# One step over four PSUM banks for the tails' u of the last pair of batches

## The chip, the cores and the metric

The kernel runs on one core of a Trainium2 chip. The metric is the device time of one execution in microseconds. The engines are PE (matmuls, with its weight loads PEld), DVE and ACT (element-wise work, both read PSUM), POOL (element-wise work and DMA issue) and SP (DMA issue). PSUM has eight banks of 128 partitions by 512 float32; here they are called g0, g1, g2, o0, o1, T and X (X is two banks side by side).

## What is computed

Cosformer attention over 8 batches, 8 heads, 576 positions and 64 features a head, and behind it a mixer: a low-rank mixing over positions and two large products.

```
def phi(x, c, s):
    r = np.maximum(x, 0.0)
    return np.concatenate([r * c, r * s], axis=-1)
...
kv = np.einsum('bhsf,bhsd->bhfd', k_p, v)
num = np.einsum('bhsf,bhfd->bhsd', q_p, kv)
...
xt = x.transpose(0, 2, 1)
h = xt @ U @ V                       # U 576 x 32, V 32 x 576
u = x + h.transpose(0, 2, 1)
ch = np.maximum(u @ w_ch1, 0.0) @ w_ch2    # 512 -> 2048 -> 512
return (u + ch).astype(np.float32)
```

## The kernel before

**Tiling.** The 576 positions of a batch are four blocks of 128 and a tail of 64. The tails of two batches share one tile of 128 rows: the even batch has the lower 64 partitions, the odd one the upper. For each batch the attention gives x (512 columns), A = (x' U) as four row strips of 32 (one for each block of 128 columns), and u = x + (V-product of A). The main blocks' u is made by `u_mm` and `u_add`, the tails' u of a pair by `u_tail`; u is then transposed by a DMA from SP (`utr_dma`, L522 and L528) and goes into the first large product.

**`u_tail` (L489 to 507).** For a set of column blocks `js` it takes one PSUM bank for each, from `four_banks` (L458): the two halves of X first, then the spare banks that the caller names. For each of the two batches and each column block it issues one matmul of 32 rows by 64 columns of weights and 128 columns of data (L498), and then one DVE addition for each column block (L505), which reads the bank and writes the block of `u_tl`. `u_tl` is transposed by SP, and its reader on PE is the tails' first product (`g1_tail`, L722).

**The order of the work** is written out by hand: a list of slots (`slots`), each a bit of PE work, and thunks that are put behind a slot (`put`); `attention_plan(b)` puts the attention of batch b at slots counted from w. For the last batch w is 187 and `a_at` is 14, so the tails' u stands behind slots 210 and 212. Every engine works through its own instructions in the order in which they are issued here; the waits between engines are found from the tiles.

**What stands around slot 210.** The first product of batch 6 (and 7) is done here with seven products of quarter size in place of eight (`g1_cross`, L650 to 681; `g1_join`, L683 to 710), for column blocks p of 128. Batch 6's blocks 4 to 7 are made this way. Products 1, 6, 7 and 4 add up in half a bank called X of that group (g0 or g1), 2 in the other half (Y), and products 5 and 3 in a bank called Z, which for batch 6 is always bank T. Joins on ACT and DVE read them: P1 and P5 (ACT copies X and Z to SBUF), C11 (DVE adds P1 and Y), C22 (DVE adds P5 and X), U2 (ACT copies X), R21 and R22 (ACT), C12 (DVE adds U2 and Z, and then takes the maximum with 0, L699). So T is taken by product 5 of block p, read by P5, taken by product 3, read by C12, and taken by product 5 of block p + 1. Between two groups of such products stand eight matmuls of the second product of batch 5 (`half_part`, L894, 128 x 256), joined by `more` (DVE, L850).

The slots are: 209, products 3 and 4 of block 5 and product 6 of block 6; 210, a `half_part`; 211, products 1 and 2 of block 7 and products 5 and 7 of block 6; 212, a `half_part`; 213, products 3 and 4 of block 6 and product 6 of block 7; 214, a `half_part`; 215, products 5 and 7 of block 7. Behind slot 209 also stands half of a sum of weights (`w1_sum`, a DVE subtraction of 128 x 1024, `w_s<-w_bf,w_s` at L612) for batch 7.

In the kernel before, the tails' step behind slot 210 has column blocks 0, 1 and 2 in X and g2 (tag "s"), and the step behind slot 212 has column block 3 in X.

```
def opened(b, p):
    g1_cross(b, p, 1)
    g1_cross(b, p, 2)
    g1_join(b, p, "P1")
    g1_join(b, p, "C11")
...
of_x, of_z = CROSS[p % 2] if b == B - 1 else (("g0", "g1")[p % 2], "T")
```

Of the kernel before, what the change touches and what calls it, by code (L numbers as in the profile page):

```python
# [17 lines left out]
def kernel(  # L18
# [28 lines left out]
    def tail(b):  # L47
        lo = TS * (b % 2)
        return slice(lo, lo + TS)
# [290 lines left out]
    def kv_unit(b, hg, tag, bufs, eng=None, n=E):  # L340
        if b not in kv_sb:
            kv_sb[b] = pool.tile([P, H, E], BF16, tag="kv", bufs=2, name="kv")
        acc = ps.tile([P, 4, n], FP32, tag=tag, bufs=bufs, name="kv_ps")
        vx = v_ext
        for i in range(4):
            h = hg * 4 + i
            for c in range(5):
                nc.tensor.matmul(  # L348
                    out=acc[:, i, :],
                    lhsT=k_of(b, c, h),  # L350
                    rhs=v_tl[:, h, 0:n] if c == 4 and b < NE
                    else vx[:, c if c < 4 else 4 + b % 2, h, 0:n],
                    start=(c == 0),
                    stop=(c == 4),
                )
        cast(eng or V_, kv_sb[b][:, hg * 4 : hg * 4 + 4, 0:n], acc)
# [83 lines left out]
    def A_of(b):  # L440
        return A_sb[b % 4]
# [16 lines left out]
    def four_banks(*spare):  # L458
        t = ps.tile([P, 2, 512], FP32, tag="X", bufs=1, name="va4_ps")
        more = [  # L460
            x if not isinstance(x, tuple)
            else ps.tile([P, 512], FP32, tag=x[0], bufs=x[1], name="va_ps")
            for x in spare
        ]
        return [t[:, 0, :], t[:, 1, :]] + more
# [3 lines left out]
    def u_mm(b, *spare, js=range(4)):  # L469
        if b not in u_bf:  # L470
            u_bf[b] = pool.tile([P, 4, 4, P], BF16, tag="u_bf", bufs=3, name="u_bf")
        va.setdefault(b, {}).update(zip(js, four_banks(*spare)))
        for c in range(4):
            for j in js:
                rows = slice(j * R, j * R + R)
                nc.tensor.matmul(  # L476
                    out=va[b][j][:, c * P : c * P + P], lhsT=V_bf[rows, c, :],
                    rhs=A_of(b)[rows, :], start=(c == 0), stop=(c == 3),
                    tile_position=(j * R, 0),
                )  # L480
# [5 lines left out]
            in1=va[b][j].rearrange("p (c n) -> p c n", c=4), op=ALU.add,  # L486
        )

    def u_tail(pr, *spare, js=range(4)):  # L489
        if pr not in u_tl:  # L490
            u_tl[pr] = pool.tile(
                [P, DM], BF16, tag="k_p" if pr == 3 else "u_tl", bufs=1, name="u_tl"
            )
        vt = dict(zip(js, four_banks(*spare)))
        for i in range(2):
            for j in js:
                rows = slice(j * R, j * R + R)
                nc.tensor.matmul(  # L498
                    out=vt[j][tail(i), 0:P], lhsT=V_tl[rows, :],
                    rhs=A_of(2 * pr + i)[rows, :], start=True, stop=True,  # L500
                    tile_position=(j * R, i * TS),
                )
        for j in js:
            ns = slice(j * P, j * P + P)
            nc.vector.tensor_tensor(  # L505
                out=u_tl[pr][:, ns], in0=x_tl[:, ns], in1=vt[j][:, 0:P], op=ALU.add
            )
# [465 lines left out]
    def loads(b):  # L973
        def thunk(dst, src):
            def go():
                if b < NE and dst is not qst:
                    load_even(dst, src, b)
                    load_odd(dst, src, b)
                    return
                load_tail(dst, src, b)  # L980
                load_main(dst, src, b)

            return go

        return thunk(qst, q), thunk(kst, k), thunk(vst, v)
# [3 lines left out]
    def spare(at):  # L989
        if at < 70:  # L990
            return ("o", 2) if 32 <= at < 52 else ("g", 3)
        return ("o", 2) if at < 86 else ("s", 1)
# [14 lines left out]
    def attention_plan(b):  # L1007

        plan = []
        if b < 4:  # L1010
            w, f_at, q_eng, k_eng, qtr, lo = PLAN[b]
        else:
            w, q_at, k_at, qtr, lo = PLAN[b]

        def put(at, f, *a, tag=False):
            if tag:
                a = a + spare(w + at)
            plan.append((w + at, lambda: f(b, *a)))

        for n, c in enumerate(QORD):  # L1020
            if b > 3:
                put(q_at[0] + q_at[1] * n, q_prep, c, q_at[2:])
                put(k_at[0] + k_at[1] * n, k_prep, c, k_at[2:])
                put(k_at[0] + (3 * n) // 2, v_prep, 0, H, (c,), (G_,))
                continue
            if b == 3:
                q_eng, k_eng = V_ if n == 3 else A_, A_ if n < 3 else None
                put((-15, -14, -13, -2, -6)[n], q_prep, c, (q_eng, q_eng))
                put(n - 12 if n < 3 else -8, k_prep, c, (A_, k_eng))
                if n > 2:  # L1030
                    put(-4, k_prep, c, (None, V_))
                put((-9, -9, -9, -7, -5)[n], v_prep, 0, H, (c,), (A_ if n > 2 else G_,))
                continue
            put(f_at + ((n - 1) % 5 if b == 2 else n), q_prep, c, (q_eng, q_eng))
            put(f_at + 6 + n, k_prep, c, (k_eng, k_eng))
            put((-5, -2, -1, -5, -5)[n], v_prep, 0, H, (c,), (V_ if n > 2 else A_,))
        for n, (c0, c1) in enumerate(((4, 5), (0, 2), (2, 4))):
            at = qtr[n] if b > 4 else -2 if b == 3 and n == 2 else qtr + 2 * n
            put(at, qtr_dma, c0, c1)
        plan.append((w + (b == 2), lambda: kv_unit(b, 0, *spare(w), A_)))  # L1040
        plan.append((w + 2, lambda: kv_unit(b, 1, *(T1 if b == 3 else spare(w + 2)), A_)))
        for n, c in enumerate(ORD):
            if b > 3:
                put((3 if b == B - 1 else 4) + 2 * n, x_unit, c, "X", 1)
            else:
                at = 4 + n if b == 3 else 4 + (3 * n) // 2
                if n % 2:
                    put(at, x_two, c, tag=True)
                else:
                    put(at, x_unit, c, "X", 1)  # L1050
        a_at = (12, 10)[b - 2] if b < 4 else 14
        if b == B - 1:
            put(a_at, A_unit, "s", 1, A_)
        else:
            put(a_at, A_unit, tag=True)
        odd = b % 2 == 1


        def two(at):
            return [T1, ("s", 1) if at >= 86 else G3] if at >= 86 or at < 64 else [spare(at)] * 2  # L1060

        if b == B - 1:
            plan.append((w + a_at + 2, lambda: u_mm(b, ("s", 1), js=(0, 1, 2))))
            plan.append((w + a_at + 5, lambda: u_mm(b, js=(3,))))
        else:
            u_at = w + a_at + (1 if b == 3 else 2)
            plan.append((u_at, lambda: u_mm(b, *two(u_at))))
        for j in range(4):
            n = (j + 1) // 2 if b == 2 else j // 2 - 1 if b == 3 else j + (2 if b > 4 and j > 1 else 0)
            put(a_at + 2 + n, u_add, j)  # L1070
        put(a_at + (2 if b == 3 else 3), utr_dma, 0, 2)
        put(a_at + (7 if b > 4 else 3 if b == 3 else 5), utr_dma, 2, 4)
        if odd:
            if b == B - 1:
                plan.append((w + a_at + 9, lambda: u_tail(b // 2, ("s", 1), js=(0, 1, 2))))
                plan.append((w + a_at + 11, lambda: u_tail(b // 2, js=(3,))))
            else:
                at = w + a_at + (10 if b == 5 else 8 if b == 3 else 9)
                plan.append((at, lambda at=at: u_tail(b // 2, *two(at))))
            put(a_at + (11 if b > 4 else 9 if b == 3 else 10), utr_dma, 4, 5)  # L1080
        for at, t in zip(lo, loads(b + 1) if lo else ()):
            plan.append((w + at, t))
        return plan
# [44 lines left out]
    T1 = ("T", 1)  # L1128
# [437 lines left out]
    for b in range(2, B):  # L1566
        for at, t in attention_plan(b):
            put(at, t)
# [37 lines left out]
```

## Time and profile before

| | |
|---|---|
| median of 3 runs | 290.36 us (290.25 to 290.58) |
| the profiled execution | 290.29 us |
| its span | 288.5 us |
| PE busy | 281.9 us, 98% |
| DVE busy | 212.0 us, 73% |
| ACT busy | 169.2 us, 59% |
| POOL busy | 64.7 us, 22% |
| granted PE clock | 0.999 |

The span runs from the first to the last event on the core; the profiled execution's own time is 1.8 us longer. Busy times of engines overlap. A row of a timeline gives the start, the length, the engine, the line and the operation, output and input names, and how many instructions were merged into the row; neighbouring instructions of one engine overlap in it, since each is shown with its whole length through the engine's pipeline. A bracket at the end of a row gives the idle time ahead of it and what ended it. The chain of work that ended last is followed back from the last instruction, and counts each stretch of time once.

### The profile page before, as it was taken

What the parts mean: (1) busy time and instruction counts of PE and PEld (TensorE: products, weight loads), DVE (VectorE), ACT (ScalarE), POOL (GpSimd) and SP (SyncE); (2) the same over time, 40 slices, a digit from 0 to 9 for tenths busy, and PEclk for the clock granted to TensorE, in tenths of its full rate; (3) what the DMA queues carried; (4) which work ended last, traced back from release to release, by engine and by line L of the source; (5) the groups of instructions that cost most, each with busy time, mean ns of one, the idle gap of its engine ahead of it and who ended that gap; (6) DMA issues with size and microseconds to landing.
All of it is one profiled execution on the core that took longest, in us unless ns stands there. A gap on an engine that the chain in (4) does not pass through costs nothing.

```text
span 288.5 us, 7416 instructions
## 1 busy us (share of the span) xinstructions
PE 281.9 (98%) x2961; PEld 199.0 (69%) x2992; DVE 212.0 (73%) x515; ACT 169.2 (59%) x347; POOL 64.7 (22%) x98
## 2 busy tenths in 40 slices
PE   8999999999999999999999999999999999999995
PEld 4785564446788546776766666766777889889884
DVE  5977858896876888557547794669968787775763
ACT  2955752177893557577735964497644556657310
POOL 6520500000046103302400501024201313303330
PEclk9999999999999999999999999999999999999999
DMA  7999999999999999998699939993930754436113
GB/s 225 306 254 250 278 160 192 225 328 220 363 252 202 272 248 256 203 332 207 175 227 268 245 74 250 180 339 91 183 77 9 140 120 82 88 96 112 39 75 143
DMA packets 92933, 56.17 MB, mean 195 GB/s; under 512 B 56580, under 2 KB 89732, under 8 KB 92900
## 3 DMA queue, kind: packets, MB, share of 16 engines
q1 hardware_dynamic: 82020, 43.41, 60.5%
q0 software_dynamic: 10688, 12.09, 20.7%
q8 instruction: 23, 0.38, 0.5%
q10 hardware_dynamic: 192, 0.20, 0.2%
q14 instruction: 10, 0.08, 0.1%
HBM read 36.86 MB, written 9.44 MB: 160 GB/s over the span
## 4 chain that ended last, share of the span: by engine, by line
PE 85%; DMA 8%; DVE 2%; ACT 2%; issue 1%; DVEq 0%; ACTq 0%
PE h_ps L894 32%; PE g_ps L580 26%; PE c_ps L677 7%; DMA kst<-in_k_dram 6%; PE o_ps L762 6%; PE gt_ps L722 5%; PE kv_ps L348 3%; PE x_ps L423 3%; DMA qst<-in_q_dram 2%; PE h_ps L762 1%; PE a_ps L446 1%; PE va_ps L476 1%; DVE k_p L309 1%; ACT q_p L307 1%; DVE v_ext L132 1%
## 5 line engine op out<-in xcount | busy, mean ns | idle before, releaser
L580 PE MATMUL g_ps<-uT,w_bf 128*128 128x512 bf16 x378 | 95.5, 379 | 1.1
L589 ACT ACTIVATE hid<-g_ps 128x512 bf16<-128x512 f32 x104 | 61.4, 597 | 59.7 <-PE g_ps L580 57.2
L580 PEld LDWEIGHTS <-w_bf 128*128 128x128 bf16 x402 | 37.5, 98 | 33.7
L894 PEld LDWEIGHTS <-hid 128*128 128x128 bf16 x560 | 53.0, 98 | 10.7
L894 PE MATMUL h_ps<-w_bf,hid 128*128 128x256 bf16 x336 | 43.1, 273 | 0.1
L894 PE MATMUL h_ps<-w_s,S 128*128 128x256 bf16 x240 | 30.4, 273 | 0.0
L894 PE MATMUL h_ps<-w_s,hid 128*128 128x256 bf16 x224 | 29.0, 273 | 0.0
L850 DVE TENSOR_TENSOR o_sb<-o_sb,h_ps 128x256 f32<-128x256 f32 (+1 forms) x38 | 16.9, 446 | 13.7 <-PE h_ps L894 11.2
L953 POOL DMA_DIRECT2D out_dram<-o_sb x20 | 12.9, 646 | 60.8 <-DVE o_sb L850 48.3
L894 PEld LDWEIGHTS <-S 128*128 128x128 bf16 x240 | 23.1, 98 | 4.9
L850 DVE TENSOR_TENSOR o_sb<-u_bf,h_ps 128x256 f32<-128x256 bf16 x32 | 13.3, 416 | 14.8 <-PE h_ps L894 14.6
L132 POOL CAST v_ext<-vst 128x512 bf16<-128x512 f32 (+1 forms) x22 | 16.0, 755 | 33.1 <-DMA vst<-in_v_dram 29.8
L484 DVE TENSOR_TENSOR u_bf<-x_bf,va_ps 128x512 bf16<-128x512 bf16 x27 | 17.6, 680 | 5.2 <-PE va_ps L476 4.1
L612 DVE TENSOR_TENSOR hid<-kept,c_ps 128x256 bf16<-128x256 f32 x36 | 14.7, 417 | 8.3 <-ACT kept L130 4.6
L952 POOL DMA_DIRECT2D o_sb<-u_bf x8 | 10.4, 1301 | 32.4 <-DVE rec L414 15.5
L130 ACT ACTIVATE kept<-c_ps 128x256 f32<-128x256 f32 x36 | 12.6, 384 | 7.2 <-PE c_ps L677 7.2
L722 PE MATMUL gt_ps<-uT_tl,w_bf 128*128 128x128 bf16 x256 | 16.2, 219 | 0.0
L433 DVE TENSOR_TENSOR x_bf<-x_ps,rec 128x512 bf16<-128x512 f32 x22 | 15.2, 692 | 0.8
L722 PEld LDWEIGHTS <-w_bf 128*128 128x128 bf16 x256 | 15.1, 98 | 0.7
L762 PE MATMUL o_ps<-w_bf,hid 128*128 128x512 bf16 x61 | 14.6, 379 | 0.3 <-issue 0.2
L130 ACT ACTIVATE o_sb<-h_ps 128x256 f32<-128x256 f32 x24 | 9.2, 381 | 9.4 <-PE h_ps L894 8.7
L307 ACT ACTIVATE k_p<-kst,cosw 128x512 bf16<-128x512 f32 x20 | 14.2, 713 | 0.1
(189 smaller groups left out, 459.5 us busy)
## 6 DMA issues: line engine op xcount, KB each, us to landing
qst<-in_q_dram SPq DMA_DIRECT2D x14, 512.0 KB, 5.8
kst<-in_k_dram SPq DMA_DIRECT2D x12, 512.0 KB, 7.4
out_dram<-o_sb POOLq DMA_DIRECT2D x21, 256.0 KB, 3.8
vst<-in_v_dram SPq DMA_DIRECT2D x10, 512.0 KB, 8.0
w_bf<-in_moe_w_ch_dram POOLq DMA_DIRECT2D x7, 512.0 KB, 13.3
out_dram<-o_sb SPq DMA_DIRECT2D x14, 256.0 KB, 2.4
kst<-in_k_dram SPq DMA_DIRECT2D x4, 640.0 KB, 7.0
o_sb<-u_bf POOLq DMA_DIRECT2D x8, 256.0 KB, 3.8
```

Source lines behind the costliest of these rows:

```text
L130: nc.scalar.activation(out=o, in_=i, func=AF.Copy, bias=0.0, scale=1.0)
L132: eng.tensor_copy(out=o, in_=i)
L307: nc.scalar.activation(out=o, in_=i, func=AF.Relu, bias=0.0, scale=w)
L433: nc.vector.tensor_tensor(out=x_of(b, c, rows).rearrange("p (g i d) -> p g i d", g=2, d=D), in0=view[:, :, :, 0:D], in1=rec[rows].unsqueez ...
L484: nc.vector.tensor_tensor(out=u_bf[b][:, j, :, :], in0=x_bf[b][:, :, ns], in1=va[b][j].rearrange("p (c n) -> p c n", c=4), op=ALU.add,)
L580: nc.tensor.matmul(out=g_ps.rearrange("p (c t) -> p c t", c=4), lhsT=w1_bf[:, d, j * P : j * P + P], rhs=uT[b][:, d, :, :], start=(d == 0) ...
L589: nc.scalar.activation(out=hid[b][:, j, :], in_=g_ps, func=AF.Relu, bias=0.0, scale=1.0)
L677: nc.tensor.matmul(out=w[to].rearrange("p (c t) -> p c t", c=2), lhsT=lhs[:, d, cs], rhs=rhs[:, d], start=(first and d == 0), stop=(d == 1 ...
L722: nc.tensor.matmul(out=g_ps[:, jj, :], lhsT=w1_bf[:, d, j * P : j * P + P], rhs=uT_tl[pr][:, d, :], start=(d == 0), stop=(d == 3),)
L762: nc.tensor.matmul(out=o[:, cols], lhsT=lhs[:, j, c * P : c * P + P], rhs=w2_bf[:, j, cols], start=(j == 0), stop=(j == NJ - 1),)
L850: eng.tensor_tensor(out=o, in0=x, in1=y, op=ALU.add)
L894: nc.tensor.matmul(out=acc, lhsT=lhs[:, j, :], rhs=rhs[:, j, :], start=(j == 0 and at is not None), stop=(j == 7), skip_group_check=at is ...
```

## The change

The last pair's tails are done in one step behind slot 210, over four banks: column blocks 0 and 1 in the two halves of X, block 2 in T, block 3 in g2. The step behind slot 212 goes. `u_tail` gets an argument that says with which block the additions begin; here they go 2, 3, 0, 1. The other three pairs are as before. Lines behind L1075 have numbers that are one lower in the changed kernel.

```
-    def u_tail(pr, *spare, js=range(4)):
+    def u_tail(pr, *spare, js=range(4), first=0):
...
-        for j in js:
+        for j in (*js[first:], *js[:first]):
             ns = slice(j * P, j * P + P)
             nc.vector.tensor_tensor(
                 out=u_tl[pr][:, ns], in0=x_tl[:, ns], in1=vt[j][:, 0:P], op=ALU.add
...
             if b == B - 1:
-                plan.append((w + a_at + 9, lambda: u_tail(b // 2, ("s", 1), js=(0, 1, 2))))
-                plan.append((w + a_at + 11, lambda: u_tail(b // 2, js=(3,))))
+                plan.append((w + a_at + 9, lambda: u_tail(b // 2, T1, ("s", 1), first=2)))
```

On PE the two matmuls of block 3 move from behind slot 212 to behind slot 210. On DVE the four additions stand together where three stood. SP's transpose of the tails keeps its place and also waits for PE's matmuls of A for batch 7. ACT and POOL have the same instructions in the same order.

## Prediction

> **What bounds the kernel now.** I read three views of the profile, in this order: the chain of work that ended last (which engine sets the end), that chain in order of time around the change (what stands on it there), and the timelines of PE, DVE and ACT over the same microseconds (who is late for whom). The whole page first:
>
> ```profile
> PE 85%; DMA 8%; DVE 2%; ACT 2%; issue 1%; DVEq 0%; ACTq 0%
> ```
>
> The DMA share belongs to the start. In the stage of the change, in order of time (start, duration, what):
>
> ```profile
> 231.09 0.87 PE h_ps L894 x8
> 231.96 0.18 PE va_ps L498 x6
> 232.15 0.98 PE c_ps L677 x8
> 233.12 0.87 PE h_ps L894 x8
> 234.00 0.17 PE va_ps L498 x2
> 234.17 0.91 PE c_ps L677 x6
> 235.08 0.87 PE h_ps L894 x8
> ```
>
> Nothing but PE stands on the chain from 214.8 to 285.0 us, but for 0.07 us of "issue". Eight 256-column matmuls take 0.87 us, at 0.109 us each, and in the stage behind the change the pieces stay at that pitch: at most 0.03 us is lost in any of them. So PE has no slack behind the change. What it loses there comes out at the end, and so does what it saves. The two L498 rows are the two steps that the change merges.
>
> PE's timeline (start, us, engine, line, what) has finer starts, by about 0.07 us earlier:
>
> ```profile
> 231.89 0.26 PE L498 MATMUL va_ps<-A_sb,V_tl 32*64 32x128 bf16 x6
> 232.08 0.61 PE L677 MATMUL c_ps<-uT,w_bf 128*128 128x256 bf16 x4
> 232.53 0.60 PE L677 MATMUL c_ps<-uT_s,w_s 128*128 128x256 bf16 x4
> 232.96 1.04 PE L894 MATMUL h_ps<-w_bf,hid 128*128 128x256 bf16 x8
> 233.93 0.24 PE L498 MATMUL va_ps<-A_sb,V_tl 32*64 32x128 bf16 x2
> 234.10 0.39 PE L677 MATMUL c_ps<-uT,w_s 128*128 128x256 bf16 x2
> 234.48 0.38 PE L677 MATMUL c_ps<-uT_s,w_bf 128*128 128x256 bf16 x2
> ```
>
> The row at 232.53 is products 5 and 7 of the crossed groups. Product 5 writes bank T, the bank that the change lends to the tails. DVE meanwhile has no idle time in its rows from 225.43 to 236.0:
>
> ```profile
> 231.50 0.41 DVE L612 TENSOR_TENSOR hid<-kept,c_ps 128x256 bf16<-128x256 f32 x1
> 231.95 0.29 DVE L699 TENSOR_SCALAR hid<-hid 128x512 bf16<-128x512 bf16 x1
> 232.16 0.68 DVE L612 TENSOR_TENSOR w_s<-w_bf,w_s 128x1024 bf16<-128x1024 bf16 x1
> 232.76 0.41 DVE L850 TENSOR_TENSOR o_sb<-o_sb,h_ps 128x256 f32<-128x256 f32 x1
> 233.09 0.68 DVE L505 TENSOR_TENSOR u_tl<-x_tl,va_ps 128x128 bf16<-128x128 bf16 x3
> 233.68 0.75 DVE L612 TENSOR_TENSOR hid<-kept,c_ps 128x256 bf16<-128x256 f32 x2
> ```
>
> The tails' additions (L505) start at 233.09, more than a microsecond after their matmuls, because three instructions of DVE's backlog are ahead of them. That delay costs nothing in the kernel before: bank T is not theirs, and product 5 waits only for C12, the row at 231.50, which ends at 231.91.
>
> **The change, part by part.**
>
> *Bank T is lent (cost).* Two T matmuls join the first step, and the addition of column block 2, which reads T, comes first of the four. Product 5 then waits in T for that addition. PE keeps its order, so behind product 5 wait product 7, the eight h_ps matmuls and all that follows. The first addition starts no earlier than the first does now, 233.09: the four DVE instructions ahead of it are the same and depend on nothing that moves. It takes 0.28 us (0.68 for three, 0.20 apart) and ends at 233.37. What passes from DVE's end to PE's start the trace shows once close by: the second L612 of the last row ends at 233.68 + 0.75 = 234.43, and the matmul of product 4, which needs it, starts at 234.48: 0.05 us. So product 5 starts at 233.42 in place of 232.53: **+0.89 us**. The price has a floor of 0.84 (no hand-over) and a ceiling of 0.93 (0.09, the hand-over from PE to ACT ahead of the kept copies at 232.78).
>
> *The tails' own wait for T.* The first matmul into T is the third of the eight and must wait for C12 to have read T: 231.91 + 0.05 = 231.96, against 231.89 for the group's start. That is up to 0.07 us, but it ends long before product 5's wait at 233.42 and is covered by it. Nothing.
>
> *The second step goes (gain).* The h_ps matmuls ahead of it start at 232.96 and hold PE for 8 x 0.109, to 233.83; product 3 starts at 234.10. So two small matmuls cost 0.27. Six cost from 231.79 (230.92 + 0.87) to 232.08, 0.29. And eight, in the first pair of batches:
>
> ```profile
> 56.27 0.38 PE L580 MATMUL g_ps<-uT,w_bf 128*128 128x512 bf16 x1
> 56.58 0.26 PE L498 MATMUL va_ps<-A_sb,V_tl 32*64 32x128 bf16 x8
> 56.78 3.41 PE L580 MATMUL g_ps<-uT,w_bf 128*128 128x512 bf16 x15
> ```
>
> The 512-column matmuls stand 0.216 apart, so PE was free at 56.49 and the eight cost 0.29. The price belongs to the group, hardly to its matmuls: merging saves **0.27 us** and adds none. Its bounds: 0.10 (what the group idles ahead of its first matmul) to 0.29. The Trainium skill has two rules here. "TensorEngine Tiling (Array Packing)", Instruction Overhead, gives a matmul some 60 cycles; by that alone the two would be worth 0.05 us (estimate from the page), and the sum below would be +0.68. The same page's Key Properties say that a change of tiling mode drains the engine, a price for each group; the rows (0.27, 0.29 and 0.29 for two, six and eight) side with that one.
>
> *Product 4's wait (gain).* Product 3 starts at 234.10 and holds PE for 0.22, to 234.32, but product 4 starts at 234.48: 0.16 us lost to C22, the second L612 of 233.68, which stood behind the three additions. In the changed kernel PE arrives later. Product 3 starts at 233.42 + 0.44 (products 5 and 7) + 0.87 = 234.73, product 4 is due at 234.95. Is C22 in time? Product 5's two matmuls end at 233.42 + 0.11 + 0.27 = 233.80; ACT copies them (P5) from 233.89 to 234.27; the four additions end at 233.97, C11 runs from 233.88 to 234.29; C22 then runs from 234.30 to 234.71 and lets PE go at 234.76, 0.19 before it is due. So the 0.16 goes: **-0.16 us**, bounds 0 and -0.16.
>
> *What else moves.* The last addition ends 1.0 us earlier (233.97 for 234.96), and SP's transpose of the tails (L528, 234.99 now) starts as much earlier; its reader is the tail product (L722) at 261.6, so nothing. On SP it stands behind the same transposes (the last starts at 231.61); its added wait is for A's matmuls of 223, long done. The L850 additions and the POOL transfer at 235.07 come about half a microsecond later with PE; nothing on the chain reads them. DVE has the same work in all, and 0.73 us of idle time at 236.0 that takes up its shift.
>
> *Sum.* +0.89 - 0.27 - 0.16 = **+0.46 us**. The profiled execution took 290.29 us (span 288.5, 1.8 around it), 0.07 under the median of 290.36. So 290.75 on its own base, and 290.82 on the median's, which I give as **290.8**, 0.16% slower. About 0.2% (0.58 us) is what a measurement of this kernel can tell from no change, so the forecast falls within it, near its edge at 290.94.
>
> **The rivals.**
>
> *Product 4 waits again (slower).* C22 needs P5, P5 needs product 5, and that now starts when DVE lets it. If the chain from product 5 over ACT and DVE takes 0.19 us longer than I worked out, product 4's wait comes back. It decides at 234.90: a C22 that ends later costs PE all that it is late. Then the 0.16 isn't regained, and up to 0.13 more is paid: +0.62 to +0.75, 291.0 to 291.1. For it: ACT and DVE work in the program's order, and C22 stands behind the copy P5 and behind C11, which wait themselves. Against it: ACT is idle for 1.02 us before 234.46.
>
> *The wait is hidden (faster side).* If DVE's backlog were shorter by 0.85 us in a run, the addition would end before product 5 is due at 232.58, and only the savings were left: -0.27 - 0.16 = -0.43, 289.9. Against it: DVE's rows have no gap for six microseconds ahead of the addition. For it: only that DVE's rows were idle 1.73 us before 225.43.
>
> *The trade comes out even (no change).* If half of that backlog were gone, product 5's wait would be about 0.45 us, the size of the two savings, and the time 290.3 to 290.5. The same speaks against it.
>
> *A second stall further on (slower).* The shift could meet a due time that I take for slack, hid sums at 239 for one: +0.9 or more, 291.3.
>
> **How the numbers follow.** Forecast 0.58 (its own range 290.5 to 291.1, a third of it above 290.94); product 4 waits again 0.20; hidden 0.07; even 0.07; a second stall 0.08. Slower by over 0.2%: 0.19 + 0.20 + 0.08 = 0.47, less 0.04 because the first rival's low end lies near the edge: 0.43. Faster by over 0.2% (under 289.78): half of the hidden case, 0.04. Within: the rest, 0.53. The range leaves out the hidden case and the worst stalls: 290.3 to 291.3.
>
> **What would show it.** In the changed kernel's timeline: eight L498 matmuls in one row near 231.9 and none near 234; four L505 additions from about 233.1; a gap of some 0.8 us on PE ahead of product 5, ended by DVE L505; product 4 right behind product 3. The last matmul starts its hand-over at about 285.5 in place of 285.02. I am wrong if the gap is missing or much under 0.8, if PE still waits ahead of product 4, or if a new gap stands behind 236.

## The result, and the profile after

The changed kernel took 291.50 us in the median of six runs (291.03 to 292.49), the kernel before 290.31 in six (290.22 to 290.58). The ratio is 1.0044, interval 1.0027 to 1.0062: slower by 1.2 us, where 0.46 was forecast, and 0.2 us outside the range. The profiled execution took 291.03 us, with a span of 289.2 us (before: 290.29 and 288.5). Single executions ran at a lower granted clock and took one to two per cent longer; medians and ratios in this document leave them out.

The page's chain of work, by engine:

```profile
PE 73%; DMA 12%; DVE 6%; ACT 5%; issue 2%; SPq 1%; ACTq 0%; DVEq 0%
```

PE's share fell from 85 to 73%. The span is only 0.7 us longer, so this isn't 12% of new waiting: followed back from the end, the chain now leaves PE at one place, and then runs on through other engines. The chain in order of time shows the place:

```profile
230.64 1.20 DVE u_bf L484 x2
231.84 0.34 DVE hid L612
...
232.41 0.68 DVE w_s L612
233.10 0.33 DVE o_sb L850
233.43 0.21 DVE u_tl L505
233.64 0.04 issue
233.68 0.60 PE c_ps L677 x4
234.28 0.87 PE h_ps L894 x8
235.15 0.66 PE c_ps L677 x6
```

In order of time these are C12 (L612), `w_s`, L850, a tails' addition (L505) and product 5 (L677): DVE's backlog and one addition now release PE. PE's timeline of the same stretch:

```profile
231.18 1.04 PE L894 MATMUL h_ps<-w_s,hid 128*128 128x256 bf16 x8
232.15 0.33 PE L498 MATMUL va_ps<-A_sb,V_tl 32*64 32x128 bf16 x8
232.41 0.61 PE L677 MATMUL c_ps<-uT,w_bf 128*128 128x256 bf16 x4
233.68 0.60 PE L677 MATMUL c_ps<-uT_s,w_s 128*128 128x256 bf16 x4 [0.66 <-DVE u_tl L505]
234.12 1.04 PE L894 MATMUL h_ps<-w_bf,hid 128*128 128x256 bf16 x8
234.99 0.38 PE L677 MATMUL c_ps<-uT,w_s 128*128 128x256 bf16 x2
235.21 0.38 PE L677 MATMUL c_ps<-uT_s,w_bf 128*128 128x256 bf16 x2
```

Eight small matmuls stand in one row, product 5 waits for DVE L505, product 4 follows product 3 by 0.22 us with no gap. The bracket's 0.66 counts from the modelled end of the last matmul; from the moment at which PE could have gone on (232.41 + 0.44 = 232.85) the wait is 0.83. DVE in the same stretch:

```profile
232.41 0.68 DVE L612 TENSOR_TENSOR w_s<-w_bf,w_s 128x1024 bf16<-128x1024 bf16 x1
233.01 0.41 DVE L850 TENSOR_TENSOR o_sb<-o_sb,h_ps 128x256 f32<-128x256 f32 x1
233.35 0.87 DVE L505 TENSOR_TENSOR u_tl<-x_tl,va_ps 128x128 bf16<-128x128 bf16 x4
234.14 0.86 DVE L612 TENSOR_TENSOR hid<-kept,c_ps 128x256 bf16<-128x256 f32 x2
235.19 0.42 DVE L850 TENSOR_TENSOR o_sb<-o_sb,h_ps 128x256 f32<-128x256 f32 x1 [0.19 <-PE h_ps L894]
```

All of these starts are later than in the kernel before by 0.26 us *ahead of* the change too: the h_ps row at 231.18 stood at 230.92. So two amounts must be kept apart. I compared the start of every weight load with the same one in the trace of before, counted from the first: the offset is 0.00 us at 80 us, 0.25 at 95 and 0.26 at 231.4; behind the changed steps, at 236, it is 0.73 and stays so to the end. The difference over the changed stretch, **0.47 us**, is what I call *local* below. The 0.26 arose between 80 and 95 us, where both kernels have the same instructions.

### The profile page after: what moved, and what is told of

Its sections match the earlier page's. It is cut to its first block, busy times and chain, and to the rows that moved or that the text cites. A ratio compares the mean times of both kernels' runs of the same rounds, so it can differ in the third digit from the quotient of the medians.

```text
span 289.2 us, 7416 instructions
## 1 busy us (share of the span) xinstructions
PE 281.9 (97%) x2961; PEld 199.2 (69%) x2992; DVE 213.2 (74%) x515; ACT 169.3 (59%) x347; POOL 64.2 (22%) x98
## 4 chain that ended last, share of the span: by engine, by line
PE 73%; DMA 12%; DVE 6%; ACT 5%; issue 2%; SPq 1%; ACTq 0%; DVEq 0%
PE h_ps L894 26%; PE g_ps L580 23%; PE c_ps L677 6%; DMA vst<-in_v_dram 5%; PE o_ps L762 4%; DMA qst<-in_q_dram 4%; PE gt_ps L722 4%; PE x_ps L423 2%; PE kv_ps L348 2%; DMA uT<-u_bf 2%; ACT k_p L307 2%; ACT q_p L307 1%; PE h_ps L762 1%; SPq L392 1%; DVE u_bf L484 1%
## 5 line engine op out<-in xcount | busy, mean ns | idle before, releaser
L850 DVE TENSOR_TENSOR o_sb<-o_sb,h_ps 128x256 f32<-128x256 f32 (+1 forms) x38 | 16.8, 445 | 13.7 <-PE h_ps L894 11.1
L850 DVE TENSOR_TENSOR o_sb<-u_bf,h_ps 128x256 f32<-128x256 bf16 x32 | 13.3, 416 | 14.7 <-PE h_ps L894 14.6
L612 DVE TENSOR_TENSOR hid<-kept,c_ps 128x256 bf16<-128x256 f32 x36 | 14.8, 417 | 8.4 <-ACT kept L130 4.7
L130 ACT ACTIVATE kept<-c_ps 128x256 f32<-128x256 f32 x36 | 12.7, 385 | 8.0 <-PE c_ps L677 7.9
L130 ACT ACTIVATE o_sb<-h_ps 128x256 f32<-128x256 f32 x24 | 9.1, 380 | 9.4 <-PE h_ps L894 8.7
```

The lines of the kernel that those rows point to most:

```text
L130: nc.scalar.activation(out=o, in_=i, func=AF.Copy, bias=0.0, scale=1.0)
L850: eng.tensor_tensor(out=o, in0=x, in1=y, op=ALU.add)
```

## The experiments

All local numbers are against the one trace of the kernel before. Where several profiles of one version are named, they come from runs on different chips (the chip of `after` isn't on record).

**The same two kernels again.** `rep_after`, `rep_after2` and `rep_after3` are the changed kernel. `null_before`, `null_before2` and `null_before3` are the kernel before with the new argument of `u_tail` in its text, unused, so that the instructions are those of before:

```
-    def u_tail(pr, *spare, js=range(4)):
+    def u_tail(pr, *spare, js=range(4), first=0):
...
-        for j in js:
+        for j in (*js[first:], *js[:first]):
```

> The changed kernel once more. Theory A (the change costs what the wait in bank T costs, +0.46 us from 231 us on, and the rest of the 1.2 us that its median lost comes from input transfers that landed late ahead of 231 us): +0.46 us behind 231 us in the profile again, whatever the offset ahead of it; the median between 290.8 and 291.5. Rival B (the wait passes on a lateness of DVE that varies from run to run, and that the kernel before hides): the local difference behind 231 us is well over 0.46 us in this profile if its time is over 291.2, with nothing late ahead of 231 us.

> The kernel before with the new argument of u_tail in the text, unused: the same instructions. Both theories: 290.3 us, within 0.2 us. If it is 0.3 us or more off, a program's time can differ by that much with no instruction changed, and that much of the 1.2 us needs no cause in the change.

> The changed kernel again, beside the next run, whose instructions are those of the kernel before. Open is only where its median's other 0.7 us came from. Theory A (they lie ahead of 231 us and fall on any program): between 231 and 236 us the profile shows +0.47 us again, the offset ahead of it differs from the two earlier profiles, and the medians of this run and of the next are about 0.5 us apart, 0.3 to 0.8. Rival B (the change costs about 1.2 us): about 1.2 us apart.

> The kernel before with the unused argument, again. Theory A: nothing between 231 and 236 us; offsets ahead of it as chance has them; the median within 0.3 us of the kernel before's.

> The changed kernel a third time, for the 0.7 us of its first median that the profiles do not place behind 231 us. If they fall on any program: +0.47 us between 231 and 236 us, and the median 0.2 to 0.8 us over the runs of the kernel before. If the change brings them: 1.0 us or more over them.

> The kernel before's instructions a third time: nothing between 231 and 236 us, and the median within 0.3 us of the kernel before's, whatever its profile shows ahead of 231 us.

| | local, us | offset at 231.4, us | median, us | ratio to before, interval |
|---|---|---|---|---|
| after | +0.47 | 0.26 | 291.50 | 1.0044 (1.0027 to 1.0062) |
| rep_after | +0.47 | 0.87 | 291.6 | 1.0016 (0.9995 to 1.0037) |
| rep_after2 | +0.47 | 0.63 | 291.4 | 1.0023 (1.0003 to 1.0042) |
| rep_after3 | +0.47 | 1.07 | 291.9 | 1.0022 (0.9998 to 1.0045) |
| null_before | 0.00 | 1.16 | 290.7 | 0.9996 (0.9974 to 1.0017) |
| null_before2 | 0.00 | 2.19 | 291.0 | 1.0010 (0.9988 to 1.0032) |
| null_before3 | -0.01 | 1.70 | 291.9 | 1.0016 (0.9994 to 1.0039) |

The local cost is the same to 0.01 us in four profiles. What stands ahead of it is not: 0.3 to 2.2 us, and the three largest offsets belong to the kernel before's own instructions. The first form of rival B, a wait that passes on a varying lateness of DVE, falls with the four equal local numbers. Over the three repeats, 35 runs of the changed kernel have a median of 291.76 us and 36 of the null kernels one of 291.32: 0.45 us apart (the means 0.37 us, resampled 95% interval 0.03 to 0.73). The same three series hold 100 runs of the kernel before itself, with a median of 290.90 us; against these the mean of the changed kernel is 0.66 us higher (0.40 to 0.93). Both intervals contain the 0.47 of the traces and neither contains 1.2, so the second form of rival B, that the change costs 1.2 us, falls in the pooled runs. They can't size the cost more closely: the null kernels, with the same instructions as the kernel before, differ from it by 0.29 us in the mean. The single medians are rougher than I had expected of them: `rep_after2` and `null_before2` are 0.40 apart, `rep_after` and `null_before` 0.9, `rep_after3` and `null_before3` 0.0. Three expectations of a median were missed: `rep_after` (291.64, over 291.5), `null_before` (0.4 over 290.3) and `null_before3` (0.5 over the runs of the kernel before beside it).

Two places carry most of these offsets, but for `null_before3`, where 0.8 of the 1.70 us arose between 10 and 40 us. The first is the opening, where PE multiplies zeros to warm up. Windows of those instructions alone (stretch, its length, PE busy and how many, PEld busy and how many, granted clock, DMA share, GB/s), first of the kernel before, then of `null_before2`:

```profile
5.00:6.00 1.00, 1.00 (x6) 0.44 (x5) 1.00 1.05 388
6.00:7.00 1.00, 1.00 (x35) 0.97 (x34) 1.00 0.98 322
```

```profile
5.00:6.00 1.00, 1.00 (x4) 0.44 (x3) 1.00 1.05 390
6.00:7.00 1.00, 1.00 (x4) 0.31 (x3) 1.00 0.98 309
```

From 6 to 7 us the kernel before runs 35 of them and `null_before2` 4; the 35 are nearly all of the short, 64-column kind that follows the first 14, which `null_before2` hasn't reached. Start to start, a 512-column matmul takes 0.427 us at first and 0.216 afterwards; the change of pace comes at the tenth of them in the profile of before and only with the last of the 14 in `null_before2`. The clock column shows 1.00 in both, so it doesn't report this. The Trainium skill's page "TensorE: Matmul & The Clock Gate", Part 1, says that the clock starts at half rate and is released by a window of about 3.4 us of activity that runs free of the kernel's start, so that the number of slow matmuls differs from run to run. These traces agree in the half pace and in the differing number, but its length wasn't near 3.4 us each time: from 1.19 us to 5.0 in the profile of before and to 7.1 in `null_before2`, 3.8 and 5.9 us of activity, and to 4.1, 2.9 us, in `adds_first2` below.

The pace alone doesn't set what the opening costs. `w1late_before` (below) has only 7 slow matmuls, fewer than the kernel before's 9, and is 1.16 us late at 20 us, because its first q input landed later (ACT could start on it at 8.10 us, in the profile of before at 6.94) and PE waited for that:

```profile
8.88 2.29 PE L378 MATMUL t_ps<-ident,q_p 128*128 128x128 bf16 x32 [1.19 <-ACT q_p L307]
```

The second place is 75 to 88 us, where inputs of batch 3 land late in some executions. ACT, then PE, in `null_before2`:

```profile
78.31 0.72 ACT L307 ACTIVATE q_p<-qst,cosw 128x512 bf16<-128x512 f32 x1 [1.55 <-DMA qst<-in_q_dram]
```

```profile
81.90 0.40 PE L446 MATMUL a_ps<-x_bf,U_bf 128*32 128x128 bf16 x16
83.64 1.03 PE L894 MATMUL h_ps<-w_s,S 128*128 128x256 bf16 x8 [1.35 <-ACT s_sb L130]
```

ACT waits 1.55 us for a transfer, its later copy of an h_ps bank (L130) comes 2.23 us later than in the profile of before, 0.70 of which is the opening's, and PE waits for that bank. In the profile of before ACT has no such wait, and the same two rows of PE stand at 81.20 and 81.53. In `after` the same wait of ACT is there, 0.30 us long, and with it come the 0.26 us by which its profile was late ahead of the change:

```profile
76.36 0.72 ACT L307 ACTIVATE q_p<-qst,cosw 128x512 bf16<-128x512 f32 x1 [0.30 <-DMA qst<-in_q_dram]
```

**The parts of the change, one at a time.** `keep2` is the wait alone: both steps stay, block 2 has bank T.

```
-    plan.append((w + a_at + 9, lambda: u_tail(b // 2, ("s", 1), js=(0, 1, 2))))
+    plan.append((w + a_at + 9, lambda: u_tail(b // 2, T1, js=(0, 1, 2), first=2)))
     plan.append((w + a_at + 11, lambda: u_tail(b // 2, js=(3,))))
```

> The wait alone: the two steps stay, but the first has column blocks 0 and 1 in X and block 2 in T, whose addition comes first. If the loan of T is the whole cost, product 5 starts 0.89 us late; the second group of matmuls (0.27) stays; product 4 no longer waits (0.16). Against the kernel before: +0.73 us between 231 and 236 us in the profile. If the merging itself costs something, it is less than that.

Local: +0.75. Ratio 1.0032 (1.0010 to 1.0054). Its profiled execution took 296.27 us and was 5.23 us late at 231.4 us already, which the local number, taken from there on, doesn't contain. Product 5 waits, and product 4 follows product 3 by 0.23 us:

```profile
238.65 0.60 PE L677 MATMUL c_ps<-uT_s,w_s 128*128 128x256 bf16 x4 [0.67 <-DVE u_tl L505]
240.23 0.39 PE L677 MATMUL c_ps<-uT,w_s 128*128 128x256 bf16 x2
240.46 0.38 PE L677 MATMUL c_ps<-uT_s,w_bf 128*128 128x256 bf16 x2
```

The loan of T is the whole cost, and the second step, which `after` hasn't, is worth 0.28 us (0.75 - 0.47).

`notwait` is the other half: one step, no loan. Block 2 of the last pair's tails is left unmultiplied, and its addition reads block 3's bank.

```
-        vt = dict(zip(js, four_banks(*spare)))
+        vt = dict(zip((0, 1, 3) if pr == 3 else js, four_banks(*spare)))
+        if pr == 3:
+            vt[2] = vt[3]
         for i in range(2):
-            for j in js:
+            for j in (0, 1, 3) if pr == 3 else js:
...
-                plan.append((w + a_at + 9, lambda: u_tail(b // 2, T1, ("s", 1), first=2)))
+                plan.append((w + a_at + 9, lambda: u_tail(b // 2, ("s", 1), first=2)))
```

> One step with four additions, but T isn't lent: column block 2 of the last pair's tails is not multiplied, and its addition reads block 3's bank, so block 2 of the tails' u is wrong; six matmuls, no wait of product 5. By the rival on record (the wait hidden: only savings left) 0.43 us less than before, 289.9. By theory A2, that DVE's backlog is the bound here in any case, product 4 waits for C22, which stands behind four additions: C22 ends 0.2 us later than before, product 4 starts 0.2 us later than before, and the time is 290.5 us, 0.2 over before.

Local: +0.20; ratio 0.9996 (0.9970 to 1.0023), too wide to tell 0.2 us, so the trace decides. Two lines were added above, so lines there are higher by 2:

```profile
232.14 0.26 PE L500 MATMUL va_ps<-A_sb,V_tl 32*64 32x128 bf16 x6
232.33 0.61 PE L679 MATMUL c_ps<-uT,w_bf 128*128 128x256 bf16 x4
232.78 0.60 PE L679 MATMUL c_ps<-uT_s,w_s 128*128 128x256 bf16 x4
233.22 1.04 PE L896 MATMUL h_ps<-w_bf,hid 128*128 128x256 bf16 x8
234.09 0.38 PE L679 MATMUL c_ps<-uT,w_s 128*128 128x256 bf16 x2
234.93 0.38 PE L679 MATMUL c_ps<-uT_s,w_bf 128*128 128x256 bf16 x2 [0.46 <-DVE hid L614]
```

Product 5 (232.78) waits for nothing, and product 4 (234.93) starts 0.62 us after PE was free (234.09 + 0.22), because C22 stands behind four additions in DVE's queue, where it stood behind three in the kernel before. Merging the steps *without* the wait, and with DVE's backlog as it is, is slower than not merging them.

`first0` puts the additions in the order 0, 1, 2, 3:

```
-                plan.append((w + a_at + 9, lambda: u_tail(b // 2, T1, ("s", 1), first=2)))
+                plan.append((w + a_at + 9, lambda: u_tail(b // 2, T1, ("s", 1))))
```

> The changed kernel with the additions in the order 0, 1, 2, 3, so that T is read third. Theory (product 5 waits for the one addition that reads T): two additions more ahead of it, 0.20 us each: +0.87 us between 231 and 236 us against the kernel before, 0.40 over the changed kernel. If PE waits for all four in any order: the same as the changed kernel, +0.47.

Local: +0.87, ratio 1.0024 (0.9999 to 1.0049). PE waits for the one addition that reads T:

```profile
235.45 0.60 PE L677 MATMUL c_ps<-uT_s,w_s 128*128 128x256 bf16 x4 [1.05 <-DVE u_tl L505]
```

The change of order in the diff is worth 0.40 us.

**The backlog.** `w1late_after` and `w1late_before` move the half sum of weights from behind slot 209 to behind slot 213, in the changed kernel and in the kernel before:

```
-        (1, 1, -8), (2, 1, -6), (3, 1, -4), (1, 0, -3), (4, 1, -2), (3, 0, -1), (2, 0, 11), (4, 0, 23),
+        (1, 1, -8), (2, 1, -6), (3, 1, -4), (1, 0, -3), (4, 1, -2), (3, 0, -1), (2, 0, 11), (4, 0, 27),
```

> The changed kernel with the half sum of weights (0.60 us on DVE) moved from behind slot 209 to behind slot 213, so that the tails' additions come 0.60 us earlier. If DVE's backlog sets product 5's wait: the first addition at about 0.6 us less after the start of the eight tails' matmuls, product 5's wait 0.2 us in place of 0.83, 0.6 us less than the changed kernel and 0.14 us less than before: 290.2 us with no late transfers. If the wait is set by something else (the matmuls of the tails, a hand-over): the gap stays at 0.8 us.

> The kernel before with the half sum of weights behind slot 213 in place of 209. Theory (DVE's backlog holds C22, and C22 holds product 4): C22 comes 0.6 us earlier and product 4's wait of 0.16 us goes: -0.16 us between 231 and 236 us. If that gap was no wait for DVE but PE's own: no difference.

Local: -0.13 and -0.15; ratios 0.9998 (0.9981 to 1.0015) and 0.9999 (0.9973 to 1.0025). In `w1late_after` product 5 starts 0.22 us after PE is free (233.06 + 0.44):

```profile
233.06 0.61 PE L677 MATMUL c_ps<-uT,w_bf 128*128 128x256 bf16 x4
233.72 0.60 PE L677 MATMUL c_ps<-uT_s,w_s 128*128 128x256 bf16 x4
```

0.60 us less DVE work ahead of the additions takes 0.60 us off the changed kernel. In the kernel before the same move takes off product 4's wait.

**A version that loses less around the change than either kernel.** `adds_first` is `w1late_after` with the half_part's addition (L850) issued behind the tails' additions; `joins_first` issues it still later, behind C11 and C22.

```
-            more(o2, hi)
+            if (b, n) == (5, 1):
+                behind.append(lambda: more(o2, hi))                        # adds_first
+                todo.setdefault(211, []).append(lambda: more(o2, hi))      # joins_first, in its place
+            else:
+                more(o2, hi)
```

> The changed kernel with the half sum of weights behind slot 213, and DVE's addition of the half_part behind slot 210 issued after the tails' four additions. The first tails' addition then starts as soon as its matmuls end, about 0.45 us after the group starts; product 5 waits under 0.05 us, and product 4 waits about 0.06 us for C22, which DVE reaches after the moved addition: -0.29 us between 231 and 236 us against the kernel before. By the rival that the second group's 0.27 us isn't saved but spent elsewhere: no difference.

> The version with the half sum late and the tails' additions ahead of the half_part's addition, again: -0.28 us between 231 and 236 us as in its first profile, the median 0.1 to 0.5 us under the run of the kernel before's instructions.

> As adds_first, with the half_part's addition moved once more, behind C11 and C22 of slot 211. If the rest of product 4's wait in adds_first is C22 behind that addition, product 4 starts right behind product 3: 0.06 us less, -0.34 us between 231 and 236 us against the kernel before. If ACT's copy P5 sets it: no difference, -0.28.

> The fastest version again: -0.34 us between 231 and 236 us; the median 0.1 to 0.6 us under the kernel before's.

Local: -0.28 and -0.29 for the first, -0.34 and -0.35 for the second. Ratios to before: 0.9984 (0.9960 to 1.0008) and 0.9990 (0.9972 to 1.0008); 0.9986 (0.9965 to 1.0007) and 0.9989 (0.9970 to 1.0008). All four are below 1, none clear of it by itself; that this version is faster rests on the traces. The median of `adds_first2` lay 0.63 us under that of `null_before2`, where 0.1 to 0.5 was expected. In `joins_first` no row of PE waits from the tails to product 4:

```profile
232.06 0.33 PE L498 MATMUL va_ps<-A_sb,V_tl 32*64 32x128 bf16 x8
232.32 0.61 PE L677 MATMUL c_ps<-uT,w_bf 128*128 128x256 bf16 x4
232.78 0.60 PE L677 MATMUL c_ps<-uT_s,w_s 128*128 128x256 bf16 x4
233.22 1.04 PE L894 MATMUL h_ps<-w_bf,hid 128*128 128x256 bf16 x8
234.09 0.38 PE L677 MATMUL c_ps<-uT,w_s 128*128 128x256 bf16 x2
234.31 0.38 PE L677 MATMUL c_ps<-uT_s,w_bf 128*128 128x256 bf16 x2
```

So the four-bank step can be had at a gain, once DVE serves PE's needs in PE's order. Not all of the gain is the step's: the later half sum alone gave the kernel before -0.15 (`w1late_before`), so the step adds 0.13 to 0.20 us to it. The moved L850 was not tried in the kernel before; in `w1late_before` PE has no wait left there that it could shorten.

## Why the prediction was right and wrong

- **Bank T is lent, +0.89: right.** The trace shows it with one addition ahead of PE (`first0` with three: 0.40 more) and with the price of DVE's backlog (`w1late_after`: 0.60 less).
- **The second step goes, -0.27, and product 4's wait, -0.16: right inside the sum.** With product 4's saving alone the sum is +0.73, and `keep2` measured 0.75; with both savings it is +0.46, and 0.47 was measured.
- **The rivals with a shorter backlog: right in direction, a little too good.** `w1late_after` takes 0.60 us of DVE's work from ahead of the additions; by the sum that is -0.14, and -0.13 was measured. `adds_first` and `joins_first` take 0.93 us, more than the 0.85 of "the wait is hidden", and measured -0.28 to -0.35 for -0.43: the tails' own wait for T, 0.07, is no longer covered, and in `adds_first` product 4 still waits 0.06. The two savings aren't there whatever becomes of the wait, though. `notwait` takes the wait away and leaves the backlog, and shows +0.20: PE comes to product 4 early, and C22 isn't there. With that backlog, product 4's saving exists only because product 5 is late.
- **"Product 4 waits again" and "a second stall further on": didn't happen.** C22 ended at 235.00 (234.14 + 0.86) and product 4, due at 235.21, started at 235.21. The offset of 0.73 at 236 us is the same at the end.
- **The step that failed is the last one of the sum: "290.82 on the median's".** It took the base, 290.36 us with three runs within 0.33, as fixed, and the range, 290.3 to 291.3, had room for the terms of the change only. The base isn't fixed: the same instructions came 0 to 2.2 us late at 231 us. The term left out is that spread, and it is larger than the whole effect. The three runs also were low ones: they and the three taken with the result all lie at 290.58 or below, and of the 100 later runs of the same kernel only 27 do, with a median of 290.90. On that base the sum gives 291.4, over the range's upper end. The three repeats put the ratio at 1.0016 to 1.0023, about the edge of 0.2% near which the forecast stood; the first six runs stood beyond it. The edge itself is no fixed thing either: the null kernels' ratios go up to 1.0016 with no instruction changed.
- **What stays open:** one of the first six runs of the changed kernel has a profile (0.47 local and 0.26 ahead). Why the other five were 0.3 to 1.5 us longer still, while six runs of the kernel before lay within 0.4 us, no trace shows. That it was time ahead of 231 us, as in the other profiles, is argued and not shown.

## What to carry to other kernels

A PSUM bank that is lent is free again only when the engine that empties it gets to it: price the loan by that engine's queue at that moment, and not by the length of the instruction that reads the bank. Where two engines are both full, savings on one of them don't add up: work out when the other is ready for each step, in the version with the cost and in the version without it. And put the spread of the base into the range, by profiles from more than one chip if there are any.

## What the runs showed of the hardware that I had not expected

- A group of 32-row matmuls among 128-row ones costs PE 0.27 to 0.29 us, whether it has two, six or eight of them, as the prediction's rows say; the merged step of eight, whose third matmul waits for T, cost 0.36 (231.18 + 0.87 to 232.41), 0.07 more, as worked out. Six with T (`keep2`) also cost 0.36, six without T (`notwait`) 0.28.
- PE's opening at half pace lasted from 7 (`adds_first2`) to 14 matmuls (`null_before2`) of 0.427 us in different executions of programs with the same opening, 0.21 us more for each, and the granted clock read 1.00 in the views of these stretches. Together with the landing of the first input this left the profiles between 0.12 us early and 1.20 us late at 20 us.
- The local times of a stretch repeated to 0.01 us between profiles of different chips, while the medians of twelve runs of the same instructions lay between 290.7 and 291.9 on three chips, and up to 0.5 us from that of the kernel before's runs on the same chip.
